# Attention and squared-ReLU FFN on one core: a finer tile of attention weights, named PSUM banks, all engines in program order, a shorter weight conversion and chunk sums on two engines

## The chip, the cores and the metric

One core of one Trainium2 chip (trn2). The metric is the device time of one execution in microseconds, as the median of several runs. All runs here were of state fast: one core runs alone, and the executions of a kernel lay within 0.6% of each other. Engines are called PE (TensorE matmul), PEld (its weight load), DVE (VectorE), ACT (ScalarE), POOL (GpSimd) and SP (SyncE, which here issues the loads and stores).

## The reference, cut to what matters

```python
batch, n_heads, seq, head_dim = (8, 12, 448, 64)          # q, k, v
# attention: RMS norm of q and k with gains g_q, g_k, softmax(q k^T / 8) v
q_n, k_n = (rmsnorm(q, g_q), rmsnorm(k, g_k))
scores = scale * np.matmul(q_n, k_n.transpose(0, 1, 3, 2))
...
x = attn_out.transpose(0, 2, 1, 3).reshape(B * S, H * D)   # 3584 x 768
# FFN
h = np.maximum(x @ w_in, 0.0)                              # 768 x 2048
return (h * h @ w_out).astype(np.float32)                  # 2048 x 768
```

The two FFN weights are float64 in memory. The kernel has to turn them into float32 itself, from pairs of 32-bit words.

## The kernel before

A batch has six pairs of heads, and a pair has four steps (the 448 rows in four chunks of 112). In a step the kernel computes the scores of one chunk for both heads ("weigh": scores on PE, exp on ACT, running sums of the exps on POOL) and one chunk of attention times V for the previous pair ("attend"). Beside this runs the FFN of the previous batch as a stream of "pieces" of 6 or 8 matmul instructions. The program also converts 56 weight chunks, 24 of w_in and 32 of w_out. Only PE is held to program order; a scheduler orders the other engines and assigns buffer slots.

```python
ps_sc = tile_pool(bufs=4, space=PSUM)     # transposes and scores
ps_av = tile_pool(bufs=2, space=PSUM)     # attention times V, and the sums' broadcast "den"
ps_mm = tile_pool(bufs=2, space=PSUM)     # FFN

def weigh(i, m):
    if m == 0:
        for e in range(2):                # one tile per head, all four chunks in it
            weights[i, e] = att.tile([CP, NJ, S], F32, name="wT", tag="wT", bufs=3)
    ...
    for e in range(2):
        sc = ps_sc.tile([CP, S], F32, name="sc", tag="sc")
        nc.tensor.matmul(sc, lhsT=kT[r, ts(m, CP)], rhs=qT[r, :], ...)
    for e, sc in enumerate(scs):
        nc.scalar.activation(weights[i, e][:, m, :], sc, AF.Exp, ...)

def to_float32(dst, low, high):           # 5 passes on DVE, 3 on POOL, 1 on ACT
    ...

with tc.manual_schedule(engines={PE}):
    ...
    for i, (b, c) in enumerate(pairs):
        normalize(i + 1)                  # squares, reduce, rr = ms ** -0.5 on POOL, qn on POOL
        for n in range(NJ):
            weigh(i, n)
            attend(i - 1, n)
            if n == 2: turn(i + 1)        # transposes of Q and K, drained as qT (DVE) and kT (ACT)
            if n == 3: load(i + 2)
            ... FFN pieces, then weight chunks (56 over 36 steps)
```

## Time and profile before

| | before |
|---|---|
| median of the 3 first runs | 1989.45 us |
| PE busy, share of the span | 1755.0 us, 88% |
| DVE, ACT, POOL busy | 496.4, 423.6, 823.0 us |
| mean granted PE clock | 0.932 |
| first FFN matmul starts at | 237.22 us |
| gap in the FFN matmuls at the start of batches 2 to 7 | 21.1 to 24.0 us |

The shares in the first two rows hide two regimes, so they are of little use by themselves. In the start, up to some 400 us, weights are converted and PE waits. Afterwards PE is the limit. The prediction below shows the lines for both. In such lines the first number is the start in us, the second the duration, then engine, source line, operation, written and read tiles, shapes and count; the bracket is the idle time of that engine before it and what ended it.

### The profile page before, as it was taken

How to read it: one execution, taken by the hardware profiler on the slowest of the kernel's cores; microseconds unless marked ns; L12 is line 12 of the kernel's file. 1: busy time of each engine (PE TensorE's matmuls, PEld its weight loads, DVE VectorE, ACT ScalarE, POOL GpSimd, SP SyncE). 2: the span in 40 equal slices, each digit the busy share in tenths (PEclk: the TensorE clock that was granted, in tenths of full speed). 3: DMA queues.
4: the chain of work that ended last, by engine and by line, in shares of the span. 5: the costliest groups of instructions: out<-in, count | busy, mean ns of one | idle time of the engine just before them, and what ended most of it. 6: DMA issues, size and time to landing. Idle time of an engine off the chain costs nothing.

```text
span 1987.5 us, 14446 instructions
## 1 busy us (share of the span) xinstructions
PE 1755.0 (88%) x5440; PEld 800.5 (40%) x5440; DVE 496.4 (25%) x602; ACT 423.6 (21%) x741; POOL 823.0 (41%) x814
## 2 busy tenths in 40 slices
PE   4446767999999999999999999999999999999998
PEld 1111223443444434444444434444444434444555
DVE  5896766212111121112111121112111121011000
ACT  3222212222221122212221122212221122211100
POOL 6988877433432244423442244423442244411200
PEclk8566688999999989999999999999999999999999
DMA  5321223001000110001000110001000110000000
GB/s 170 104 84 51 83 80 86 23 27 44 15 14 22 30 36 24 19 22 39 19 14 22 30 36 23 19 22 39 19 14 22 30 36 24 10 8 17 0 9 26
DMA packets 80532, 70.25 MB, mean 35 GB/s; under 512 B 48196, under 2 KB 69700, under 8 KB 80452
## 3 DMA queue, kind: packets, MB, share of 16 engines
q1 hardware_dynamic: 80128, 69.23, 12.3%
q8 instruction: 45, 0.74, 0.1%
q14 instruction: 35, 0.29, 0.0%
q10 hardware_dynamic: 324, 0.00, 0.0%
HBM read 58.20 MB, written 11.01 MB: 35 GB/s over the span
## 4 chain that ended last, share of the span: by engine, by line
PE 78%; DVE 3%; ACT 2%; POOL 0%; issue 0%; DMA 0%; ACTq 0%; POOLq 0%
PE yps L304 30%; PE hps L275 27%; PE sc L184 10%; PE av L232 8%; PE tr L163 2%; PE den L239 2%; ACT wT L187 2%; DVE qT L165 1%; DVE rden L249 1%; DMA words<-in_moe_w_out_dram 0%; POOL w_out_sb L388 0%; POOL words L387 0%; ACT kT L169 0%; DVE w_out_sb L370 0%; DVE w_out_sb L374 0%
## 5 line engine op out<-in xcount | busy, mean ns | idle before, releaser
L275 PE MATMUL hps<-xT,w_in_sb 128*128 128x448 f32 x1536 | 604.1, 549 | 6.3 <-ACT h L284 6.3
L304 PE MATMUL yps<-w_out_sb,h 128*128 128x384 f32 x1792 | 594.2, 489 | 0.0
L304 PEld LDWEIGHTS yps<-w_out_sb,h 128*128 128x128 f32 x1792 | 335.5, 190 | 255.1 <-issue 35.0
L275 PEld LDWEIGHTS hps<-xT,w_in_sb 128*128 128x128 f32 x1536 | 289.2, 192 | 308.5 <-issue 297.9
L201 POOL TENSOR_TENSOR sum<-sum,wT 112x448 f32<-112x448 f32 x192 | 220.5, 1148 | 349.3 <-ACT wT L187 342.2
L187 ACT ACTIVATE wT<-sc,rr 112x448 f32<-112x448 f32 x384 | 227.6, 633 | 623.5 <-PE sc L184 528.5
L184 PE MATMUL sc<-qT,kT 64*112 64x448 f32 x768 | 284.6, 657 | 68.8 <-ACT wT L187 50.3
L249 DVE RECIPROCAL rden<-den 128x448 f32<-128x448 f32 x48 | 141.9, 2956 | 476.1 <-PE den L239 476.1
L201 POOL TENSOR_TENSOR sum<-wT 112x448 f32<-112x448 f32 x96 | 110.4, 1150 | 313.7 <-PE den L239 222.5
L232 PE MATMUL av<-wT,vt 112*64 112x448 f32 x768 | 209.5, 628 | 0.0
L184 PEld LDWEIGHTS sc<-qT,kT 64*112 64x112 f32 x768 | 78.8, 191 | 245.1 <-ACT wT L187 116.9
L284 ACT ACTIVATE h<-hps 128x448 f32<-128x448 f32 x128 | 69.4, 542 | 373.6 <-PE hps L275 373.6
L137 POOL TENSOR_TENSOR rr<-ms,minus_half 112x16 f32<-112x16 f32 x48 | 141.3, 2943 | 11.7 <-DVE ms L133 10.9
L294 POOL TENSOR_TENSOR h<-h 128x448 f32<-128x448 f32 x64 | 59.5, 932 | 187.7 <-ACT h L284 187.7
L132 DVE TENSOR_REDUCE ms<-squares 112x8 f32<-112x512 f32 x96 | 65.6, 684 | 203.8 <-ACT squares L131 194.8
L289 POOL TENSOR_TENSOR h<-h 128x384 f32<-128x384 f32 x64 | 52.9, 827 | 146.8 <-ACT h L284 146.8
L163 PE MATMUL tr<-ident,qk 112*128 112x112 f32 x192 | 32.1, 295 | 91.5 <-DVE qT L165 91.5
L232 PEld LDWEIGHTS av<-wT,vt 112*64 112x64 f32 x768 | 41.4, 146 | 148.4 <-issue 148.4
L311 DVE COPY y<-yps 128x384 f32<-128x384 f32 x28 | 15.6, 556 | 289.2 <-PE yps L304 289.2
L165 DVE TENSOR_SCALAR qT<-tr,g 128x448 f32<-128x448 f32 x48 | 32.1, 669 | 215.5 <-PE tr L163 215.5
L131 ACT ACTIVATE squares<-qk 112x512 f32<-112x512 f32 x96 | 60.3, 628 | 104.0 <-DMA qk<-in_q_dram 49.6
L253 DVE TENSOR_TENSOR xT<-av,rden 128x448 f32<-128x448 f32 x48 | 29.9, 623 | 200.2 <-PE av L232 177.5
(40 smaller groups left out, 691.7 us busy)
## 6 DMA issues: line engine op xcount, KB each, us to landing
words<-in_moe_w_in_dram SPq DMA_DIRECT2D x24, 512.0 KB, 3.9
words<-in_moe_w_out_dram SPq DMA_DIRECT2D x32, 384.0 KB, 3.1
qk<-in_q_dram SPq DMA_DIRECT2D x48, 224.0 KB, 2.9
vt<-in_v_dram SPq DMA_DIRECT2D x48, 224.0 KB, 2.6
qk<-in_k_dram SPq DMA_DIRECT2D x96, 112.0 KB, 3.1
out_dram<-y SPq DMA_DIRECT2D x8, 336.0 KB, 2.8
out_dram<-y SPq DMA_DIRECT2D x8, 288.0 KB, 2.7
out_dram<-y SPq DMA_DIRECT2D x8, 240.0 KB, 2.6
```

The costliest lines, as they stand in the source:

```text
L131: nc.scalar.activation(squares, qk[:, x], AF.Square)
L132: nc.vector.tensor_reduce(out=ms[:, ts(x, 2 * NJ)], in_=squares, axis=AX.X, op=ALU.add)
L137: nc.gpsimd.tensor_tensor(out=rr.rearrange("p x r -> p (x r)"), in0=ms, in1=minus_half.to_broadcast([CP, 4 * NJ]), op=ALU.pow,)
L163: nc.tensor.transpose(tr[:, ts(j, CP)], rows[:, j].rearrange("p h d -> p (h d)"), ident[:CP, :CP])
L184: nc.tensor.matmul(sc, lhsT=kT[r, ts(m, CP)], rhs=qT[r, :], start=True, stop=True)
L187: nc.scalar.activation(weights[i, e][:, m, :], sc, AF.Exp, scale=normal[i][2][:, 2 * m + e : 2 * m + e + 1])
L201: nc.gpsimd.tensor_tensor(out=sums[i, e], in0=so_far, in1=wT[:, m, :], op=ALU.add)
L232: nc.tensor.matmul(av[ds(e * D, D), :], lhsT=vt[:, e, m, :], rhs=weights[i, e][:, m, :], start=m == 0, stop=m == NJ - 1,)
L249: nc.vector.reciprocal(out=rden, in_=den)
L275: nc.tensor.matmul(ps, lhsT=w_in_sb[:, c, ts(f, P)], rhs=xT[c], start=c == 0, stop=c == NC - 1,)
L284: nc.scalar.activation(h[:, at : at + S], ps, AF.Relu)
L304: nc.tensor.matmul(ps, lhsT=h2[f][:, ts(n, P)], rhs=w_out_sb[:, f, ts(half, HALF)], start=f == 0, stop=f == NF - 1,)
```

## The change

Its intent: PE should find its PSUM banks free, no engine should be ordered by a guess, the weights should cost fewer passes, and POOL should be relieved. It does these things. (The tiles that PE's matmuls write stand in PSUM, which the kernel uses as eight banks of 512 values per partition; the other tiles stand in SBUF.) PSUM tiles become eight named banks. The wT tile is cut into one tile per chunk (12 of them, the same bytes). All engines are held to program order. The weight conversion gets three passes on ACT, one on POOL and three on DVE. The second head's sums go to DVE. V is loaded apart from Q and K, each pair is normalized after its forerunner's first step, and the weight chunks come one per step in batch 0 and three per step after it. Within a step the order is now weight chunks, FFN pieces, weigh, attend, and the FFN stream starts at step 4 of a batch instead of after step 5.

```diff
+    banks = [psum.tile([P, 512], F32, name=f"bank{n}") for n in range(8)]
...
-            tr = ps_sc.tile([P, S], F32, name="tr", tag="sc")
+            tr = banks[2 + x][:, 0:S]
...
+    def new_weights(i, m):
+        for e in range(2):
+            weights[i, e, m] = att.tile([CP, S], F32, name="wT", tag="wT", bufs=3 * NJ)
...
-            sc = ps_sc.tile([CP, S], F32, name="sc", tag="sc")
+        scs = [banks[2 * (m % 2) + e][:CP, 0:S] for e in range(2)]
...
-            nc.gpsimd.tensor_tensor(out=sums[i, e], in0=so_far, in1=wT[:, m, :], op=ALU.add)
+            engine = nc.gpsimd if e == 0 else nc.vector
+            engine.tensor_tensor(out=sums[i, e], in0=so_far, in1=weights[i, e, m], op=ALU.add)
...
+        nc.scalar.activation(high.bitcast(F32), high.bitcast(F32), AF.Copy, scale=REBIAS)
+        nc.scalar.activation(low.bitcast(F32), low, AF.Copy, scale=2.0**-29, bias=2.0**23)
+        nc.scalar.activation(low, low.bitcast(F32), AF.Copy, bias=-(2.0**23))
+        nc.gpsimd.tensor_scalar(out=high.bitcast(F32), ..., op0=ALU.min, op1=ALU.max)
+        nc.vector.tensor_scalar(out=bits, in0=high, ...shift left 4, right 1)
         nc.vector.scalar_tensor_tensor(out=bits, in0=high, scalar=0x80000000, in1=bits, ...)
-        (of the old passes: four on DVE, three on POOL, one on ACT)
+        nc.vector.tensor_tensor(out=bits, in0=bits, in1=low, op=ALU.add)
...
-    with tc.manual_schedule(engines={PE}):
+    with tc.manual_schedule(engines=ENGINES):
...
+                for _ in range(1 if b == 0 else len(chunks) if shift else 3):
+                    if chunks:
+                        load_weights(*chunks.popleft())
+                while ... done * (steps - NJ) < pieces * (step - NJ + 1):
+                    next(stream, None)
                 weigh(i, n)
+                attend(i - 1, n)
+                if n == 0: normalize(i + 1)
                 if n == 2: turn(i + 1)
+                if n == NJ - 1: load_v(i + 1)
```

More of the change, by code (lines that the diff above doesn't have):

```diff
@@ L16 @@
 AX = mybir.AxisListType
-PE = mybir.EngineType.PE
+ENGINES = set(mybir.ALL_ENGINES)
 P = 128
 NJ = 4
-FEW = 2.0**-15
-MOST = (2.0 - 2.0**-3 - 2.0**-23) * 2.0**15 * 2.0
-WEIGHT_STEPS = 36
+REBIAS = 2.0**-112
+MOST = (2.0 - 2.0**-3 - 2.0**-23) * 2.0**-96
 MOST_G = 7.5
@@ L91, in program @@
     ffn_p = ctx.enter_context(tc.tile_pool(name="ffn", bufs=2))
-    ps_sc = ctx.enter_context(tc.tile_pool(name="ps_sc", bufs=4, space=bass.MemoryType.PSUM))
-    ps_av = ctx.enter_context(tc.tile_pool(name="ps_av", bufs=2, space=bass.MemoryType.PSUM))
-    ps_mm = ctx.enter_context(tc.tile_pool(name="ps_mm", bufs=2, space=bass.MemoryType.PSUM))
+    psum = ctx.enter_context(tc.tile_pool(name="psum", bufs=1, space=bass.MemoryType.PSUM))
     ident = const.tile([P, P], F32, name="ident")
@@ L102, in program, with load_qk @@
     w_out_sb = const.tile([P, NF, DM], F32, name="w_out_sb")
+    banks = [psum.tile([P, 512], F32, name=f"bank{n}") for n in range(8)]
     pairs = [(b, c) for b in range(B) for c in range(NPAIR)]
-    loaded, normal, turned, weights, sums, avs, xts = {}, {}, {}, {}, {}, {}, {}
-    def load(i):
+    loaded, values, normal, turned, weights, sums, dens, xts = {}, {}, {}, {}, {}, {}, {}, {}
+    def load_qk(i):
         b, c = pairs[i]
         qk = io.tile([CP, 2, 2 * NJ, D], F32, name="qk", tag="qk")
-        vt = io.tile([CP, 2, NJ, D], F32, name="vt", tag="vt", bufs=3)
-        for dst, src in ((qk[:, 0], q), (vt.rearrange("p h j d -> p (h j) d"), v)):
-            nc.sync.dma_start(
-                dst.rearrange("p (h j) d -> p h (j d)", j=NJ),
-                src[b, 2 * c : 2 * c + 2].rearrange("h (p j) d -> p h (j d)", j=NJ),
-            )
+        nc.sync.dma_start(
+            qk[:, 0].rearrange("p (h j) d -> p h (j d)", j=NJ),
+            q[b, 2 * c : 2 * c + 2].rearrange("h (p j) d -> p h (j d)", j=NJ),
+        )
         for e in range(2):
@@ L122, in load, with load_v @@
             )
-        loaded[i] = qk, vt
+        loaded[i] = qk
+    def load_v(i):
+        b, c = pairs[i]
+        vt = io.tile([CP, 2, NJ, D], F32, name="vt", tag="vt")
+        nc.sync.dma_start(
+            vt.rearrange("p h j d -> p h (j d)"),
+            v[b, 2 * c : 2 * c + 2].rearrange("h (p j) d -> p h (j d)", j=NJ),
+        )
+        values[i] = vt
     def normalize(i):
-        qk = loaded[i][0]
+        qk = loaded.pop(i)
         ms = small.tile([CP, 4 * NJ], F32, name="ms", tag="ms", bufs=2)
@@ L170, in turn @@
         turned[i] = qT, kT
+    def new_weights(i, m):
+        for e in range(2):
+            weights[i, e, m] = att.tile([CP, S], F32, name="wT", tag="wT", bufs=3 * NJ)
     def weigh(i, m):
-        if m == 0:
-            for e in range(2):
-                weights[i, e] = att.tile([CP, NJ, S], F32, name="wT", tag="wT", bufs=3)
         if shift:
             return weigh_shifted(i, m)
+        new_weights(i, m)
         qT, kT = turned[i]
-        scs = []
-        for e in range(2):
+        scs = [banks[2 * (m % 2) + e][:CP, 0:S] for e in range(2)]
+        for e, sc in enumerate(scs):
             r = ds(e * D, D)
-            sc = ps_sc.tile([CP, S], F32, name="sc", tag="sc")
             nc.tensor.matmul(sc, lhsT=kT[r, ts(m, CP)], rhs=qT[r, :], start=True, stop=True)
-            scs.append(sc)
         for e, sc in enumerate(scs):
             nc.scalar.activation(
-                weights[i, e][:, m, :], sc, AF.Exp, scale=normal[i][2][:, 2 * m + e : 2 * m + e + 1]
+                weights[i, e, m], sc, AF.Exp, scale=normal[i][2][:, 2 * m + e : 2 * m + e + 1]
             )
@@ L196, in add_up @@
         for e in range(2):
-            wT = weights[i, e]
             if m == 1:
                 sums[i, e] = att.tile([CP, S], F32, name="sum", tag="sum", bufs=2)
-            so_far = wT[:, 0, :] if m == 1 else sums[i, e]
-            nc.gpsimd.tensor_tensor(out=sums[i, e], in0=so_far, in1=wT[:, m, :], op=ALU.add)
+            so_far = weights[i, e, 0] if m == 1 else sums[i, e]
+            engine = nc.gpsimd if e == 0 else nc.vector
+            engine.tensor_tensor(out=sums[i, e], in0=so_far, in1=weights[i, e, m], op=ALU.add)
     def weigh_shifted(i, m):
+        if m == 0:
+            for n in range(NJ):
+                new_weights(i, n)
         qT, kT = turned[i]
@@ L207, in weigh_shifted @@
             r = ds(e * D, D)
-            sc = ps_sc.tile([CP, S], F32, name="sc", tag="sc")
+            sc = banks[2 * e][:CP, 0:S]
             nc.tensor.matmul(sc, lhsT=qT[r, ts(m, CP)], rhs=kT[r, :], start=True, stop=True)
@@ L213, in weigh_shifted @@
             nc.scalar.activation(w, sc, AF.Exp, bias=nmax)
-            tr = ps_sc.tile([CP, NJ, CP], F32, name="trw", tag="sc")
+            tr = banks[2 * e + 1][:CP, 0:S].rearrange("p (n c) -> p n c", n=NJ)
             for n in range(NJ):
                 nc.tensor.transpose(tr[:, n, :], w[:, ts(n, CP)], ident[:CP, :CP])
-            nc.vector.tensor_copy(out=weights[i, e][:, :, ts(m, CP)], in_=tr)
+            for n in range(NJ):
+                nc.vector.tensor_copy(out=weights[i, e, n][:, ts(m, CP)], in_=tr[:, n, :])
         if m == NJ - 1:
@@ L224, in attend @@
         b, c = pairs[i]
-        vt = loaded[i][1]
-        if m == 0:
-            avs[i] = ps_av.tile([P, S], F32, name="av", tag="av")
-            if c == 0:
-                xts[b] = [None] * NC
-        av = avs[i]
+        vt = values[i]
+        if m == 0 and c == 0:
+            xts[b] = [None] * NC
+        av = banks[4 + i % 2][:, 0:S]
         for e in range(2):
             nc.tensor.matmul(
-                av[ds(e * D, D), :], lhsT=vt[:, e, m, :], rhs=weights[i, e][:, m, :],
+                av[ds(e * D, D), :], lhsT=vt[:, e, m, :], rhs=weights.pop((i, e, m)),
                 start=m == 0, stop=m == NJ - 1,
@@ L236, in attend @@
         if m == 1:
-            den = ps_av.tile([P, S], F32, name="den", tag="av")
+            den = banks[5 - i % 2][:, 0:S]
             for e in range(2):
@@ L249, in attend @@
                 nc.vector.reciprocal(out=rden, in_=den)
-            normal[i] = rden
+            dens[i] = rden
         if m == NJ - 1:
             xT = ffn_p.tile([P, S], F32, name="xT", tag="xT", bufs=NC + 2)
-            nc.vector.tensor_tensor(out=xT, in0=av, in1=normal.pop(i), op=ALU.mult)
+            nc.vector.tensor_tensor(out=xT, in0=av, in1=dens.pop(i), op=ALU.mult)
             xts[b][c] = xT
-            del weights[i, 0], weights[i, 1], turned[i], loaded[i], avs[i]
+            del turned[i], normal[i], values[i]
     left = {}
@@ L272, in ffn @@
         for f in range(NF):
-            ps = ps_mm.tile([P, S], F32, name="hps", tag="mm")
+            ps = banks[6 + f % 2][:, 0:S]
             for c in range(NC):
@@ L301, in ffn @@
             for half in range(2):
-                ps = ps_mm.tile([P, HALF], F32, name="yps", tag="mm")
+                ps = banks[6 + half][:, 0:HALF]
                 for f in range(NF):
@@ L353, in to_float32 @@
     def to_float32(dst, low, high):
+        nc.scalar.activation(high.bitcast(F32), high.bitcast(F32), AF.Copy, scale=REBIAS)
+        nc.scalar.activation(low.bitcast(F32), low, AF.Copy, scale=2.0**-29, bias=2.0**23)
+        nc.scalar.activation(low, low.bitcast(F32), AF.Copy, bias=-(2.0**23))
+        nc.gpsimd.tensor_scalar(
+            out=high.bitcast(F32), in0=high.bitcast(F32), scalar1=MOST, scalar2=-MOST,
+            op0=ALU.min, op1=ALU.max,
+        )
         bits = dst.bitcast(U32)
         nc.vector.tensor_scalar(
-            out=bits, in0=high, scalar1=1, scalar2=1,
-            op0=ALU.logical_shift_left, op1=ALU.logical_shift_right,
-        )
-        nc.gpsimd.tensor_scalar(
-            out=dst, in0=dst, scalar1=MOST, scalar2=FEW, op0=ALU.min, op1=ALU.max
-        )
-        nc.vector.tensor_scalar(
-            out=bits, in0=bits, scalar1=4, scalar2=1,
+            out=bits, in0=high, scalar1=4, scalar2=1,
             op0=ALU.logical_shift_left, op1=ALU.logical_shift_right,
@@ L377, in to_float32 @@
         )
-        nc.vector.tensor_scalar(
-            out=high, in0=bits, scalar1=0x40000000, scalar2=0xFF800000,
-            op0=ALU.bitwise_xor, op1=ALU.bitwise_and,
-        )
-        nc.vector.tensor_scalar(
-            out=bits, in0=bits, scalar1=0x40000000, scalar2=None, op0=ALU.bitwise_xor
-        )
-        power, rest = high.bitcast(F32), low.bitcast(F32)
-        nc.scalar.activation(rest, low, AF.Copy, scale=2.0**-52)
-        nc.gpsimd.tensor_tensor(out=rest, in0=rest, in1=power, op=ALU.mult)
-        nc.gpsimd.tensor_tensor(out=dst, in0=dst, in1=rest, op=ALU.add)
-    load(0)
+        nc.vector.tensor_tensor(out=bits, in0=bits, in1=low, op=ALU.add)
+    load_qk(0)
     for e in range(2):
@@ L399, in program @@
     make_identity(nc, ident)
-    load(1)
-    stream, pieces, done, start = iter(()), 0, 0, 0
+    load_qk(1)
+    load_v(0)
+    steps = NPAIR * NJ
     chunks = deque(weight_chunks())
-    n_chunks = len(chunks)
-    with tc.manual_schedule(engines={PE}):
+    with tc.manual_schedule(engines=ENGINES):
         normalize(0)
         turn(0)
+        stream, pieces, done = iter(()), 0, 0
         for i, (b, c) in enumerate(pairs):
-            if i + 1 < len(pairs):
-                normalize(i + 1)
+            if i + 2 < len(pairs):
+                load_qk(i + 2)
             for n in range(NJ):
+                step = c * NJ + n
+                if step == NJ and b:
+                    stream, pieces, done = ffn(b - 1), ffn_pieces(b - 1), 0
+                for _ in range(1 if b == 0 else len(chunks) if shift else 3):
+                    if chunks:
+                        load_weights(*chunks.popleft())
+                while shift and step == NJ and done < pieces or done * (steps - NJ) < pieces * (step - NJ + 1):
+                    next(stream, None)
+                    done += 1
+                if shift and n == 0 and i:
+                    for m in range(NJ):
+                        attend(i - 1, m)
                 weigh(i, n)
-                if i:
+                if i and not shift:
                     attend(i - 1, n)
-                if n == NJ - 1 and c == 0 and i:
-                    stream, pieces, done = ffn(b - 1), ffn_pieces(b - 1), 0
-                    start = NJ if b > 1 else WEIGHT_STEPS - NPAIR * NJ - 12
+                if n == 0 and i + 1 < len(pairs):
+                    normalize(i + 1)
                 if n == 2 and i + 1 < len(pairs):
                     turn(i + 1)
-                if n == NJ - 1 and i + 2 < len(pairs):
-                    load(i + 2)
-                step = c * NJ + n
-                last = NPAIR * NJ - 1
-                while done * (last - start) < pieces * (step - start):
-                    next(stream, None)
-                    done += 1
-                ready = min(n_chunks, n_chunks * (b * NPAIR * NJ + step + 1) // WEIGHT_STEPS)
-                while n_chunks - len(chunks) < ready:
-                    load_weights(*chunks.popleft())
+                if n == NJ - 1 and i + 1 < len(pairs):
+                    load_v(i + 1)
             if c == NPAIR - 1:
```

## The prediction

> **What bounds the kernel now.** I read the page's slices first. They show two regimes. Up to about 400 us POOL and DVE are loaded and PE is not. After that PE is at 9 in every slice. So I asked for the engines' busy time in four stretches. The first ends where the first FFN matmul starts (237.22 us in PE's timeline). The second ends at 400 us, when the weights are in and PE has filled up. The third ends where the attention of the last batch is done.
>
> ```profile
> core 0: us, PE busy (x) PEld busy (x) DVE busy (x) ACT busy (x) POOL busy (x), PEclk, DMA share, GB/s
> 0.00:237.00 237.00, 115.79 (x296) 36.27 (x296) 178.08 (x228) 65.86 (x115) 195.96 (x167) 0.66 0.33 99
> 237.00:400.00 163.00, 125.47 (x348) 54.73 (x348) 82.48 (x125) 38.73 (x71) 104.39 (x121) 0.85 0.23 64
> 400.00:1840.00 1440.00, 1372.66 (x4390) 631.58 (x4390) 233.60 (x245) 309.51 (x538) 507.81 (x504) 0.98 0.09 24
> 1840.00:1987.00 147.00, 141.11 (x412) 77.91 (x410) 2.23 (x4) 9.47 (x18) 14.80 (x24) 0.99 0.04 12
> ```
>
> Row 1: POOL works 196 of 237 us and DVE 178, PE's clock is 0.66. This is the conversion of the 56 weight chunks (37 of them in batch 0, by the code's 56/36 per step) beside batch 0's attention. Row 3: PE is busy 1373 of 1440 us, so here only PE's own gaps and stretched matmuls can be won. PE's timeline of one ordinary pair shows them:
>
> ```profile
> 866.82 0.97 PE L232 MATMUL av<-wT,vt 112*64 112x448 f32 x4
> 867.73 0.60 PE L163 MATMUL tr<-ident,qn 112*128 112x112 f32 x4
> 869.11 0.60 PE L163 MATMUL tr<-ident,qk 112*128 112x112 f32 x4 [0.78 <-DVE qT L165]
> 869.55 7.92 PE L304 MATMUL yps<-w_out_sb,h 128*128 128x384 f32 x24
> 877.40 1.00 PE L184 MATMUL sc<-qT,kT 64*112 64x448 f32 x2
> 879.12 1.00 PE L184 MATMUL sc<-qT,kT 64*112 64x448 f32 x2 [0.72 <-ACT wT L187]
> 880.06 0.97 PE L232 MATMUL av<-wT,vt 112*64 112x448 f32 x4
> ```
>
> K's transposes wait until Q's have been drained, and the second head's scores wait for the first head's exp. With four score buffers neither should wait. ScalarE's timeline of the same pair gives the reason:
>
> ```profile
> 846.68 0.63 ACT L187 ACTIVATE wT<-sc,rr 112x448 f32<-112x448 f32 x1 [3.03 <-PE sc L184]
> 856.39 0.63 ACT L187 ACTIVATE wT<-sc,rr 112x448 f32<-112x448 f32 x1 [9.09 <-PE sc L184]
> 866.93 0.63 ACT L187 ACTIVATE wT<-sc,rr 112x448 f32<-112x448 f32 x1 [9.90 <-PE sc L184]
> ...
> 878.44 0.63 ACT L187 ACTIVATE wT<-sc,rr 112x448 f32<-112x448 f32 x1 [3.56 <-PE sc L184]
> 881.12 2.21 ACT L187 ACTIVATE wT<-sc,rr 112x448 f32<-112x448 f32 x4 [2.05 <-PE av L232]
> ```
>
> Only one exp runs per step, then four in a row once the previous pair's last av is done. The wT tile holds a head's four chunks and has three buffers for two heads per pair, so the second head's tile is the one that the previous pair still reads. Its scores of three steps sit in three of the four score banks, and everything else shares one. That is my reading of the root: SBUF buffer size, seen as a PSUM shortage.
>
> **What the Trainium skill says.** "Perfetto Trace Analysis", section Optimization Strategy: the same gap repeating on the engine that should be saturated can mean too little SBUF or PSUM for the next tile. The trace agrees: 0.72 and 0.78 us recur in every pair. "PSUM — Partial Sum Buffer", section Engine vs sequencer instructions: ScalarE, VectorE and GpSimd queues are strict FIFO, so program order decides what stands behind a wait. The trace agrees: ScalarE stood 99.0 us in all behind weight DMAs, with exps queued. "SBUF — State Buffer", section Who interferes with whom: a two-port VectorE operation and GpSimd exclude each other. The trace agrees: line 363 on 128x512 took 413 ns at best and 828 at the median. "TensorE: Matmul & The Clock Gate", section What's actually happening: an idle PE falls to half clock. Here the four score matmuls of a step take 1.01 us in the full stage and 1.84 in the sparse one.
>
> **The change, part by part.**
>
> (1) Finer wT tiles (12 of one chunk, same bytes) and fixed banks. A slot now comes back from the attend two steps earlier, and Q's and K's transposes have banks 2 and 3. Saved per ordinary pair: 0.78 us (K's wait), and for the last step's scores 880.06-877.40 = 2.66 us becomes 0.94 (the start-to-start of an undivided pair, 866.82-865.89), so 1.72. Sum 2.5 us. There are five such pairs per batch: 12.5 us.
>
> (2) Start of a batch. The steps before the FFN stream begins are attention alone: six now (steps 0 to 5), four after. PE's timeline has FFN gaps of 24.0, 22.4, 22.7, 21.1, 22.7 and 21.1 us (batches 2 to 7). Six steps at full clock would take 6x1.84 (scores 0.94, av 0.90) + 2x0.85 (den) + 0.95 (transposes) = 13.7, so about 8.7 is lost. After, four steps would take 9.2, but normalize(i+1) is issued in program order after step 0: two exps 1.3, squares 0.63, reduce 0.68, squares, reduce, ms 0.2, rr 2.9, qn 1.05 and hand-overs are about 9.6 us before the transposes, against PE reaching them at 6.4. I lose 3.2 there, 0.6 for kT and an estimated 3 for half clock: 7. Saved 8.7-7 = about 1.7 us. With (1), 14 us per batch, six batches: 84 us. Two pairs of batch 1 add 5. Steady gain: 89 us.
>
> (3) Weight conversion. Removed per chunk: two or three DVE passes and POOL's two 1.0-1.4 us multiplies and adds (lines 387, 388). Left on DVE: a shift as line 363 (0.42 to 0.9), a merge as line 374 (0.68 undisturbed), an add of two tensors, which I take as 0.65: about 1.9 us against 4.65 (0.91+0.90+1.26+0.60+0.99 for 128x512). On POOL one clamp, about 0.85, against 3.57. On ScalarE three passes of 0.65 instead of one. Over 56 chunks DVE falls from 213 us to about 95 and POOL from 168 to about 42. The second head's sums (3 per pair at 1.15 on POOL) go to DVE at about 0.62, the time of line 253's same size: POOL loses 165 us over the kernel, DVE gains 89.
>
> Neither engine is then full in batch 0; the order of the queues is what costs. One pair on DVE (one chunk per step), from one qT to the next: chunk 1.9, sum 0.6 and xT 0.6 after qT (the last two wait for PE, so 4.3 together); then the next pair's first chunk. Its DMA is queued behind load_v, which waits for PE's last av (3.6 after qT at half clock), and behind load_qk: issues 0.45+0.35+1.23, landing about 4.5 later, ScalarE 0.65, POOL 0.85: DVE starts it 11.3 us after qT. Then chunk 1.9, two reduces with a squares between 2.2, ms 0.3; then DVE stands until rr 2.9, qn 1.05 and the next clamp 0.85 have gone through POOL (5); then chunk 1.9, sum 0.6, rden 2.96, chunk 1.9, sum 0.6, qT 0.7. Sum: 11.3+1.9+2.2+0.3+5+8.7 = 29 to 30 us. First chunk on DVE at about 25 us (its DMA now stands behind load_qk(2), issued at 17.8 in the trace), first qT at 40, second at 63 (that chunk's DMA is not held up), fifth of the rest at 63+4x30 = 185: batch 0 ends near 189 us.
>
> Batch 1: 32 chunks of w_out in eleven steps, in two buffers (the y tiles). A buffer's round: DMA 3.1, ScalarE 0.56, POOL 0.6, DVE 0.6+0.65+0.55, hand-overs 0.6 = 6.6, so 3.3 us per chunk, 10 to 12 per step with the pair's stalls. Four steps without FFN to about 237, seven with it to about 320. At 320: step 11, 7x56/20 = 20 FFN pieces. The old kernel at 400: step 16, 35 pieces (192 hps matmuls and 24 yps). The difference is 5 steps (11 us) and 15 pieces at 2.34 (36 us): 47, a little more as the clock recovers, so the new kernel stands there at 370. Gain 30 us.
>
> Sum: 1989.5 - 89 - 30 = 1870.
>
> **The rivals.** (a) The start wins much more: if DMA latency and POOL's chain are hidden better than I laid end to end, batch 0 could run at 24 us per pair and batch 1 at 9 per step: about 50 us more, 1820. For it: DVE's own work is only about 16 us per pair. Against: ScalarE, SP and DVE are now strictly ordered, and each pair has two round trips between them. (b) The start wins nothing or loses: ScalarE has three passes per chunk and every exp and relu stands behind three chunks whose DMA has only two buffers; at 14 us per step the FFN of batch 1 is starved and the 30 us are gone: 1900 to 1920. For it: the 99 us above. (c) Program order puts a new gap of half a microsecond into every step of the full stage (168 steps, 84 us), which would eat (1): about 1950. I went through PE's dependences there (relu two hps back, exp two steps back, y copies, den's sums from the step before) and each producer stands in its own queue before anything later than PE's own place, so I give this little. (d) POOL's relief alone shortens the full stage: no, POOL works 508 of 1440 us there and PE waits for it nowhere.
>
> **Range and chances.** The start is uncertain by some 40 us, the steady part by 20, mostly independent: 1830 to 1915. Two percent faster is below 1949.7; only (c) or a bad (b) misses it.
>
> **What would show each step.** (1) right: no gap before K's transposes, two exps per step, scores always four together; PE's period per batch 199 to 201 and 221 to 223 us instead of 213 and 235. (2) right: FFN gaps near 14 us with a wait of PE's transposes for qn. (3) right: DVE near 95 us for conversion, batch 0 ending near 190, FFN starting near 237 again, ScalarE waiting for weight DMAs. Wrong: hps or yps waiting for ScalarE or DVE in the full stage, or an FFN start later than 260 or earlier than 200.

## The result, and the profile after

The changed kernel takes 1875.73 us (median of 4 runs, 1874.19 to 1879.09); the kernel before took 1991.19 us over the 4 runs of the same series. The ratio is 0.9419, 95% interval 0.9396 to 0.9443: 5.8% faster. A ratio here is the mean time of one kernel's runs over the mean of the other's runs of the same rounds, so it is not quite the ratio of the two medians. The time lies 6 us from the predicted 1870.

The busy times of the engines in four stretches of the changed kernel, cut at the same events as those of before (columns as there):

```profile
core 0: us, PE busy (x) PEld busy (x) DVE busy (x) ACT busy (x) POOL busy (x), PEclk, DMA share, GB/s
0.00:245.00 245.00, 95.58 (x296) 33.17 (x296) 126.49 (x172) 102.65 (x184) 81.88 (x77) 0.63 0.30 93
245.00:380.00 135.00, 113.03 (x340) 49.30 (x338) 62.99 (x93) 58.02 (x113) 54.75 (x68) 0.92 0.27 77
380.00:1726.00 1346.00, 1325.73 (x4399) 623.92 (x4398) 342.10 (x366) 303.55 (x540) 399.55 (x385) 0.98 0.10 26
```

In the first row POOL fell from 196 to 82 us and DVE from 178 to 126, yet the stretch grew from 237 to 245 us. No engine is full there any more: the busiest works 126 of 245 us. In the third row PE is busy 98.5% of the time (1325.73 of 1346), against 95.3% before (1372.66 of 1440).

PE's timeline of an ordinary pair after, to set beside the one of before:

```profile
622.18 0.97 PE L244 MATMUL bank<-wT,vt 112*64 112x448 f32 x4
623.08 0.60 PE L173 MATMUL bank<-ident,qn 112*128 112x112 f32 x4
623.52 0.55 PE L173 MATMUL bank<-ident,qk 112*128 112x112 f32 x4
623.90 10.50 PE L316 MATMUL bank<-w_out_sb,h 128*128 128x384 f32 x32
634.33 1.01 PE L195 MATMUL bank<-qT,kT 64*112 64x448 f32 x4
635.27 0.97 PE L244 MATMUL bank<-wT,vt 112*64 112x448 f32 x4
```

No line has a bracket: K's transposes follow Q's at once, and the four score matmuls run together in 0.94 us from start to start. ACT's timeline of the same stretch has two exps per step, and no run of four:

```profile
622.34 1.16 ACT L197 ACTIVATE wT<-bank,rr 112x448 f32<-112x448 f32 x2 [0.52 <-PE bank L195]
624.11 0.53 ACT L179 COPY kT<-bank 128x448 f32<-128x448 f32 x1 [0.61 <-PE bank L173]
635.37 1.16 ACT L197 ACTIVATE wT<-bank,rr 112x448 f32<-112x448 f32 x2 [10.74 <-PE bank L195]
```

The start of a batch, on PE's timeline:

```profile
686.09 0.60 PE L173 MATMUL bank<-ident,qn 112*128 112x112 f32 x4 [2.97 <-POOL qn L152]
686.53 0.55 PE L173 MATMUL bank<-ident,qk 112*128 112x112 f32 x4
...
687.47 2.06 PE L195 MATMUL bank<-qT,kT 64*112 64x448 f32 x4 [0.40 <-DVE qT L175]
...
689.46 1.76 PE L244 MATMUL bank<-wT,vt 112*64 112x448 f32 x4
```

PE waits 2.97 us for qn, and then the scores take 2.06 us and the av group 1.76 instead of 1.01 and 0.97: the clock has dropped (0.63 of full speed was granted from 686 to 691 us, 1.00 before). The FFN gap is 16.1 to 16.9 us.

One pair of batch 0, on the timeline of all engines (SPq lines are DMA issues):

```profile
96.55 0.68 DVE L175 TENSOR_SCALAR qT<-bank,g 128x448 f32<-128x448 f32 x1
...
97.28 1.84 PE L195 MATMUL bank<-qT,kT 64*112 64x448 f32 x4 [9.65 <-DVE qT L175]
...
100.85 0.33 SPq L129 DMA_DIRECT2D vt<-in_v_dram  x1
...
103.07 1.98 SPq L360 DMA_DIRECT2D words<-in_moe_w_in_dram  x4
...
107.44 0.65 ACT L374 ACTIVATE words<-words 128x512 f32<-128x512 f32 x1 [7.13 <-DMA words<-in_moe_w_in_dram]
...
108.85 0.43 DVE L382 TENSOR_SCALAR w_in_sb<-words 128x512 uint32<-128x512 uint32 x1 [6.77 <-POOL words L377]
...
113.29 2.91 POOL L147 TENSOR_TENSOR rr<-ms,minus_half 112x16 f32<-112x16 f32 x1 [4.47 <-DVE ms L143]
...
117.98 1.35 DVE L382 TENSOR_SCALAR w_in_sb<-words 128x512 uint32<-128x512 uint32 x1 [4.77 <-POOL words L377]
```

This is the loop that the prediction laid end to end: qT, the scores that need it, V's load behind the last av, the next chunks' loads behind V's, ACT, POOL, DVE 11.6 us after qT ended at 97.2; then rr and qn on POOL with DVE standing 4.77 us. From one PE wait for qT to the next a pair takes 31.0, 31.5, 31.9 and 32.4 us.

**Where the time went.** I compare the two at the same state of PE. At 400.84 us the old kernel has done step 15 of batch 1 and 35 FFN pieces. The new one has done step 15 at 380.87 with 34 pieces; the missing piece is 8 matmuls of 0.33 us, so it stands there at 383.5. The start gained 17 us. From there to the end the old kernel takes 1987.5-400.8 = 1586.7 and the new one 1873.4-383.5 = 1489.9 us: 97 us. Sum 114, the difference of the two profiled spans.

### The profile page after: what moved, and what is told of

Its sections match the earlier page's. It is cut to its first block, busy times and chain, and to the rows that moved or that the text cites. A ratio compares the mean times of both kernels' runs of the same rounds, so it can differ in the third digit from the quotient of the medians.

```text
span 1873.4 us, 14405 instructions
## 1 busy us (share of the span) xinstructions
PE 1675.4 (89%) x5440; PEld 784.3 (42%) x5440; DVE 533.8 (28%) x634; ACT 473.6 (25%) x853; POOL 551.7 (29%) x558
## 3 DMA queue, kind: packets, MB, share of 16 engines
q1 hardware_dynamic: 80128, 69.23, 13.2%
## 4 chain that ended last, share of the span: by engine, by line
PE 80%; issue 5%; DVE 4%; POOL 4%; DMA 3%; ACT 2%; SPq 1%; POOLq 0%; ACTq 0%; DVEq 0%
PE bank L316 31%; PE bank L287 30%; PE bank L195 8%; PE bank L244 7%; POOL rr L147 2%; DMA words<-in_moe_w_out_dram 2%; PE bank L173 2%; PE bank L251 1%; DMA words<-in_moe_w_in_dram 1%; DVE rden L261 1%; POOL words L377 1%; DVE sum L211 1%; ACT words L374 1%; DVE w_in_sb L386 1%; DVE w_in_sb L382 1%
## 5 line engine op out<-in xcount | busy, mean ns | idle before, releaser
L287 PE MATMUL bank<-xT,w_in_sb 128*128 128x448 f32 x1536 | 612.1, 554 | 22.0 <-ACT h L296 20.7
L316 PE MATMUL bank<-w_out_sb,h 128*128 128x384 f32 x1792 | 593.9, 489 | 0.0
L316 PEld LDWEIGHTS bank<-w_out_sb,h 128*128 128x128 f32 x1792 | 335.5, 190 | 253.9 <-issue 32.2
L287 PEld LDWEIGHTS bank<-xT,w_in_sb 128*128 128x128 f32 x1536 | 291.4, 194 | 335.3 <-issue 287.6
L197 ACT ACTIVATE wT<-bank,rr 112x448 f32<-112x448 f32 x384 | 221.9, 629 | 553.9 <-PE bank L195 549.4
L195 PE MATMUL bank<-qT,kT 64*112 64x448 f32 x768 | 219.3, 638 | 101.2 <-DVE qT L175 70.6
L211 POOL TENSOR_TENSOR sum<-sum,wT 112x448 f32<-112x448 f32 x96 | 111.9, 1165 | 410.8 <-ACT wT L197 410.0
L211 DVE TENSOR_TENSOR sum<-sum,wT 112x448 f32<-112x448 f32 x96 | 109.8, 1143 | 421.3 <-ACT wT L197 421.3
L244 PE MATMUL bank<-wT,vt 112*64 112x448 f32 x768 | 200.8, 605 | 0.0
L261 DVE RECIPROCAL rden<-bank 128x448 f32<-128x448 f32 x48 | 141.5, 2948 | 1.2 <-PE bank L251 1.2
L211 POOL TENSOR_TENSOR sum<-wT 112x448 f32<-112x448 f32 x48 | 71.0, 1479 | 75.9 <-PE bank L251 74.9
L323 DVE COPY y<-bank 128x384 f32<-128x384 f32 x28 | 15.3, 548 | 229.8 <-PE bank L316 229.8
```

The costliest lines, as they stand in the source:

```text
L195: nc.tensor.matmul(sc, lhsT=kT[r, ts(m, CP)], rhs=qT[r, :], start=True, stop=True)
L197: nc.scalar.activation(weights[i, e, m], sc, AF.Exp, scale=normal[i][2][:, 2 * m + e : 2 * m + e + 1])
L211: engine.tensor_tensor(out=sums[i, e], in0=so_far, in1=weights[i, e, m], op=ALU.add)
L244: nc.tensor.matmul(av[ds(e * D, D), :], lhsT=vt[:, e, m, :], rhs=weights.pop((i, e, m)), start=m == 0, stop=m == NJ - 1,)
L261: nc.vector.reciprocal(out=rden, in_=den)
L287: nc.tensor.matmul(ps, lhsT=w_in_sb[:, c, ts(f, P)], rhs=xT[c], start=c == 0, stop=c == NC - 1,)
```

## The experiments

Twelve kernels ran, all correct, all timed in three rounds beside the kernel before (median 1989.35 to 1990.27 us in the three series). "FFN start" is the first FFN matmul and "gap" the FFN gap at the starts of the later batches, both from PE's timeline.

| kernel | median us | ratio to before [95%] | FFN start us | gap us |
|---|---|---|---|---|
| before | 1989 to 1991 | 1 | 237.2 | 21.1 to 24.0 |
| changed | 1875.73 | 0.9419 [0.9396, 0.9443] | 245.5 | 16.1 to 16.9 |
| b_wt | 1823.02 | 0.9146 [0.9116, 0.9175] | 215.7 | 13.4 |
| b_conv | 1903.68 | 0.9548 [0.9520, 0.9577] | 181.5 | 22.4 to 23.9 |
| b_wtconv | 1747.71 | 0.8788 [0.8773, 0.8803] | 164.3 | 13.4 |
| a_pools | 1816.41 | 0.9113 [0.9083, 0.9143] | 202.5 | 13.8 to 16.2 |
| a_flip | 1817.80 | 0.9138 [0.9122, 0.9153] | 204.6 | 13.8 to 16.2 |
| a_pe | 1754.69 | 0.8804 [0.8775, 0.8833] | 150.5 | 13.2 to 14.8 |
| a_sumpool | 1869.76 | 0.9383 [0.9352, 0.9414] | 239.8 | 16.1 to 16.9 |
| a_oldconv | 1912.12 | 0.9595 [0.9566, 0.9623] | 259.8 | 15.9 to 16.9 |
| a_norm | 1866.10 | 0.9365 [0.9336, 0.9394] | 240.6 | 15.9 to 16.1 |
| a_spread | 1837.72 | 0.9218 [0.9191, 0.9245] | 246.8 | none |
| a_pe_fs | 1737.44 | 0.8737 [0.8723, 0.8752] | 155.0 | none |
| a_order_best | 1742.36 | 0.8761 [0.8747, 0.8776] | 169.7 | none |

The labels say what they start from: b_ is the kernel before with a part of the change, a_ is the changed kernel with a part altered.

### b_wt: the finer wT tiles alone

```diff
-            weights[i, e] = att.tile([CP, NJ, S], F32, name="wT", tag="wT", bufs=3)
+            weights[i, e, m] = att.tile([CP, S], F32, name="wT", tag="wT", bufs=3 * NJ)
```
(and the uses of it; pools, order and conversion as before)

> The kernel before with one part of the change alone: the wT tiles cut to one chunk each (12 of them, same bytes); PSUM pools, conversion, sums and order of the engines stay as before. Theory (the second head's wT tile comes back too late and its scores hold the banks): the waits of 0.72 us (scores for exp) and 0.78 us (K's transposes for qT) go from the full stage, two exps per step; 2.5 us per ordinary pair, about 12.5 per batch plus some at the batch starts, so 80 to 95 us: 1895 to 1910 us. Rival (the rotating PSUM pool is at fault and fixed banks are needed): gaps stay, 1975 to 1995 us.

Measured: 1823.02 us, 167 us below before and 53 us below the whole change. The direction was the theory's, the size almost double its 80 to 95 us. The start of a batch on PE's timeline:

```profile
666.20 0.60 PE L163 MATMUL tr<-ident,qn 112*128 112x112 f32 x4
666.64 0.55 PE L163 MATMUL tr<-ident,qk 112*128 112x112 f32 x4
667.11 1.01 PE L186 MATMUL sc<-qT,kT 64*112 64x448 f32 x4
```

The rotating pools deliver three bank pairs in a row without a wait. The gap at a batch start is 13.4 us with the old six steps of attention, just the 13.7 us that the prediction worked out for them at full clock. So the 8.7 us that it saw lost there came from wT too. The start of one batch's FFN to that of the next takes 191.1 or 211.8 us, against 214.1 and 233.1 to 234.4: 22.2 us per batch on average. The start gained as well: from 504.0 to 461.6 us at the FFN start of batch 2, 42 us. The sum 42+124 (the rest of the spans, 1483.5 against 1360.0) is the 166 us of the profiled spans. Named banks and program order were not needed for any of it.

### a_pools: the changed kernel with rotating PSUM pools

```diff
-    banks = [psum.tile([P, 512], F32, name=f"bank{n}") for n in range(8)]
+    ps_sc, ps_av, ps_mm pools as before, with 4, 2 and 2 buffers
```

> The changed kernel with the eight named banks put back into the three rotating PSUM pools (4, 2 and 2 buffers), all else as changed. Theory: with fine wT tiles the pools rotate without waits, so within 10 us of the changed kernel, 1868 to 1886 us. Rival (named banks remove the gaps): the 0.7 and 0.8 us gaps come back and about 85 us with them, 1945 to 1965 us.

Measured: 1816.41 us, 59 us faster than the changed kernel. Both theories fell: the banks do not save, and they are not neutral; they cost. FFN starts at 202.5 instead of 245.5 us, so most of it lies in batch 0. A pool hands out four banks in turn. Scores of step 1, scores of step 2, transposes and scores of step 3 alternate between the two halves. The named version gives the scores of step m the pair m % 2, so those of step 3 take banks 2 and 3, the very banks in which Q's transposes wait for DVE to drain qT. In batch 0 DVE reaches qT late, and the score matmuls of step 3, the last av, V's load and the next chunks' loads queue up behind it (the pair shown above: 9.65 us of PE waiting).

### a_flip: named banks, dealt out in the order of use

```diff
-            tr = banks[2 + x][:, 0:S]
+            tr = banks[2 * (i % 2) + x][:, 0:S]
-        scs = [banks[2 * (m % 2) + e][:CP, 0:S] for e in range(2)]
+        scs = [banks[2 * ((i + (m == 1)) % 2) + e][:CP, 0:S] for e in range(2)]
```

> The changed kernel with its named banks dealt out otherwise: Q's and K's transposes and the score pairs alternate between the two bank pairs in the order of use, so that the last step's scores of a pair no longer need the banks that qT is drained from. Theory (the pools run was 60 us faster because in batch 0 the last step's scores, the last av and so load_v and the next chunk DMAs stood behind qT; 24 instead of 31.5 us per pair): as with pools, 1808 to 1824 us, FFN start near 202 us. Rival (the pools win in some other way, through waits released earlier than by named tiles): 1855 to 1880 us.

Measured: 1817.80 us and FFN start 204.6: as with pools. It is which bank, not named against pooled. PE's timeline in batch 0:

```profile
78.42 1.01 PE L195 MATMUL bank<-qT,kT 64*112 64x448 f32 x4
79.36 0.97 PE L244 MATMUL bank<-wT,vt 112*64 112x448 f32 x4
90.57 1.84 PE L195 MATMUL bank<-qT,kT 64*112 64x448 f32 x4 [10.23 <-DVE qT L175]
```

PE still waits for qT, but now with the scores of the next pair, which use qT as data. The last av of the pair is done at 80 us, ahead of the wait, so the loads behind it go out early. The next such wait ends at 114.47 us: a pair takes 23.9 us instead of 31 to 32.

### b_conv and b_wtconv: the conversion alone, and with wT

```diff
     def to_float32(dst, low, high):
-        (the old nine passes)
+        (the new seven passes)
```

> The kernel before with the new weight conversion alone. Its batch 0 had GpSimd busy 196 of 237 us; the new conversion takes 2.7 us of GpSimd and 2.7 us of VectorE work off each of 37 chunks there. Theory (the engines' work bounded the old start, and it is the program order that let the changed kernel keep only about 17 us of that): here the FFN starts 40 to 80 us earlier than 237 us, and the kernel takes 1910 to 1955 us. Rival (chunk buffers and DMA bound the old start): FFN start within 15 us of 237, 1970 to 1995 us.

Measured: 1903.68 us, 86 us faster, a little more than the theory's range. FFN starts at 181.5, 56 us earlier. So the engines' work did bound the old start.

> The kernel before with two parts of the change, the fine wT tiles and the new conversion, and nothing of the named banks, the program order or the split sums. Theory (these two carry the whole gain and the rest costs): the two gains of 167 and 86 us nearly add up, 1730 to 1765 us, FFN start near 150 us, gaps at the batch starts near 13.4 us. Rival (both shorten the same stretch of the start, so they do not add): 1785 to 1820 us.

Measured: 1747.71 us. The parts give 167 and 86 us alone and 242 us together, so they nearly add up. Two parts of the change, a few lines each, are worth more than twice the whole. The rest (banks, order, sums, the new order within a step, the FFN start, V's load, the place of normalize, the pace of the chunks) costs 1875.7-1747.7 = 128 us. Of these only the banks, the engines' order and the sums have runs of their own below; what the others cost is not shown.

### a_oldconv: the changed kernel with the old conversion

```diff
     def to_float32(dst, low, high):
-        (the new seven passes)
+        (the old nine passes)
```

> The changed kernel with the old weight conversion. Theory (in program order a chunk's passes lie end to end, so the shorter chain of the new one is what makes program order bearable): a pair of batch 0 goes from 31 to 32 us to about 45 to 55, a chunk of w_out from 3.3 to 5 us or more: 100 to 180 us slower, 1975 to 2055 us. Rival (DMA landing and the rr and qn chain bound the start, not the passes): less than 40 us slower, 1880 to 1915 us.

Measured: 1912.12 us, 36 us slower: the rival was right and my 100 us and more were wrong. FFN start moves by 14 us only, and the first matmul with w_out from 373.8 to 407.9 us. The new conversion is worth 86 us where queues are free and 36 us in program order, where chunk loads and the chain through rr and qn set the pace.

### a_pe: only PE in program order

```diff
-    with tc.manual_schedule(engines=ENGINES):
+    with tc.manual_schedule(engines={mybir.EngineType.PE}):
```

> The changed kernel with only PE in program order, the other engines ordered by the scheduler as before. Theory (program order is neutral in the full stage and costs time in the start, where VectorE and GpSimd stand behind DMA and the rr and qn chain): start shorter by 20 to 60 us, full stage the same, 1815 to 1860 us. Rival (program order brings part of the gain): slower than the changed kernel, 1890 to 1940 us, with waits of PE for ScalarE or VectorE in the full stage.

Measured: 1754.69 us, 121 us faster than the changed kernel. The theory's direction held and its 20 to 60 us were too few. FFN starts at 150.5 us, 95 us earlier, with the bad bank choice still in. DVE is busy 115 of the first 150 us (126 of 245 in program order). Program order brings nothing in the full stage either; it costs some 20 us there, where the theory had none: from the first w_out matmul to the end a_pe takes 1751.9-272.8 = 1479 us and the changed kernel 1873.4-373.8 = 1500.

### a_sumpool: all sums on POOL

```diff
-            engine = nc.gpsimd if e == 0 else nc.vector
+            engine = nc.gpsimd
```

> The changed kernel with all chunk sums on GpSimd again. Theory: in the full stage nothing waits for GpSimd, and in batch 0 the sums are not on the chain from qT to qT, so 0 to 10 us slower, 1872 to 1886 us. Rival (the split carries part of the gain because GpSimd was the full engine of the start): 20 us or more slower, 1895 us and up.

Measured: 1869.76 us; its ratio's interval (0.9352 to 0.9414) overlaps the changed kernel's, so the split sums save nothing, and may cost a little. The groups of the changed kernel by line (busy us, mean ns of one, then idle time before):

```profile
L211 POOL TENSOR_TENSOR sum<-sum,wT 112x448 f32<-112x448 f32 x96 | 111.9, 1165 | 410.8 <-ACT wT L197 410.0
L211 DVE TENSOR_TENSOR sum<-sum,wT 112x448 f32<-112x448 f32 x96 | 109.8, 1143 | 421.3 <-ACT wT L197 421.3
L211 POOL TENSOR_TENSOR sum<-wT 112x448 f32<-112x448 f32 x48 | 71.0, 1479 | 75.9 <-PE bank L251 74.9 <-ACT wT L197 1.0
L211 DVE TENSOR_TENSOR sum<-wT 112x448 f32<-112x448 f32 x48 | 35.2, 734 | 228.6 <-PE bank L251 227.5 <-ACT wT L197 1.1
```

The prediction took 0.62 us for a sum on DVE. Sums of two steps out of three average 1.14 us there (second line); in most of them the partner on POOL had started 0.41 us before. The first sums of a pair (third and fourth line) mostly start on both engines at once: there DVE's takes 0.63 us and POOL's 1.61 (medians), where POOL alone took 1.13 in the kernel before.

### a_norm: normalize one step earlier at a batch start

```diff
-                if n == 0 and i + 1 < len(pairs):
+                if n == 0 and (c or not i) and i + 1 < len(pairs):
                     normalize(i + 1)
+                if n == NJ - 1 and c == NPAIR - 1 and i + 2 < len(pairs):
+                    normalize(i + 2)
```

> The changed kernel, but the pair that follows the first pair of a batch is normalized one step earlier (last step of the batch before, still under FFN matmuls). Theory (the FFN gap of 16.1 us at each batch start is the 9.6 us chain squares, reduce, rr, qn, which PE's transposes wait for 3.0 us, and the half clock after it): the wait for qn goes, gap 9.5 to 11.5 us, six batches: 28 to 40 us faster, 1836 to 1848 us. Rival (half clock comes from the lack of FFN work itself, not from the wait): gap 13 to 14 us, 12 to 20 us faster, 1856 to 1864 us.

Measured: 1866.10 us, gap 15.9 to 16.1. Neither answer came, since the edit does not do what I wrote. In the changed kernel a step begins with its FFN pieces, so a normalize at the end of the batch's last step stands behind all of them: the last FFN matmul ends at 667.3 and squares begins at 669.3 us. The chain was moved ahead by one attention step, and the wait for qn fell from 2.97 to 2.08 us only. Of the 10 us in the total, 5 lie before the FFN start (240.6 against 245.5), which this edit hardly touches; a_sumpool, in another series, starts its FFN as early (239.8), so differences of this size between series are not read. This run tells nothing about the theory.

### a_spread: the FFN stream stretched over the batch start

```diff
-                while ... done * (steps - NJ) < pieces * (step - NJ + 1):
+                while done < due(pieces, (step - NJ) % steps):   # w_in pieces at the old pace,
+                                                                  # the others up to step 3 of the next batch
-            if c == NPAIR - 1:
-                for _ in stream: pass
```

> The changed kernel, but the second half of each FFN stream is stretched over the first four steps of the next batch, so that these have FFN matmuls too. Theory: no FFN gap over 3 us is left, no wait for qn, full clock; the work at full clock of a gap is 9.2 us of 16.1, so 6 to 7 us for each of six batches: 36 to 42 us faster, 1834 to 1840 us. Rival (something else, such as xT or h tiles not yet free, takes the gap's place): under 20 us faster, above 1856 us.

Measured: 1837.72 us, 38 us faster than the changed kernel and inside the range. No FFN gap is left after batch 1, PE waits for nothing after 374 us, and its clock there is 1.00. This settles that the loss at a batch start goes when PE has FFN work beside the chain through rr and qn. How much of the loss was the wait for qn and how much the lower clock, no run separates.

### a_pe_fs and a_order_best: two ways to a faster kernel

a_pe_fs is the changed kernel with the edits of a_pe, a_flip and a_spread.

> The changed kernel with only PE in program order, the alternating banks and the FFN stream stretched over the batch start: meant to beat both kernels. Theory (the three act on different places: queue order in the start, banks in the start, batch starts): 1755 minus 30 to 36 for the batch starts (five or six gaps of 14 us with 9.2 of work at full clock in them) minus 5 to 15 for the banks, 1705 to 1722 us. Rival (with free queues the banks no longer matter and the stretched stream meets late xT tiles): 1735 to 1755 us.

Measured: 1737.44 us, the fastest of all, 7.4% below the changed kernel by the medians, but 15 us above its range and inside the rival's. The stretches of this kernel (columns as above):

```profile
0.00:274.00 274.00, 187.23 (x613) 75.08 (x614) 179.15 (x267) 157.10 (x298) 157.92 (x145) 0.86 0.41 122
274.00:1588.00 1314.00, 1314.00 (x4418) 616.71 (x4417) 341.53 (x363) 306.14 (x539) 422.81 (x389) 1.00 0.10 27
```

From 274 us on PE is busy all the time at full clock; there is nothing left there but PE's own work. Stretching the stream took 18 us off that part (1479 to 1461 us from the first w_out matmul to the end), not 30: I had taken six gaps' surplus over 9.2 us each, and about 12 us of it I cannot place. The banks gave nothing here (FFN start 155.0 against 150.5), as the rival had it; its other half, late xT tiles, did not come, for PE waits for nothing after 274 us. That DVE drains qT early with free queues is my reading.

a_order_best keeps full program order but changes the program:

```diff
-        to_float32(dst, words[:, :, 0], words[:, :, 1])        # right behind its own load
+        issued.append((dst, words[:, :, 0], words[:, :, 1]))   # loads up to 4 chunks ahead
...
                 attend(i - 1, n)
+                convert(1 if b == 0 else 2)                    # passes behind the step's attention
...
-                if n == NJ - 1 and i + 1 < len(pairs): load_v(i + 1)
+                if n == 1 and i: load_v(i)
```
(with the edits of a_flip and a_spread)

> The changed kernel in full program order, but with its program reordered: chunk DMAs issued up to four chunks ahead, a chunk's passes placed after the step's attention, two chunks a step in batch 1, V loaded a pair later, alternating banks, stretched FFN stream. Theory (program order costs only by what the program puts ahead of what): a pair of batch 0 falls to about 18 to 20 us, FFN starts at 140 to 165 us, no FFN gap at batch starts; 1690 to 1740 us. Rival (strict queues on every engine cost in the start whatever the order): FFN start above 185 us, 1770 us or more.

Measured: 1742.36 us, 2 us outside the range; a pair of batch 0 takes 22.1 us (waits for qT end at 62.29, 84.39 and 106.51 us), not 18 to 20, and FFN starts at 169.7. Still, in full program order this is 133 us faster than the changed kernel. Of the 95 us that a_pe takes off the FFN start, this kernel gets 76 in full program order. So most of what the change lost in the start it lost by what its program puts ahead of what and by its banks. How much of the 22.1 us strict queues still cost I did not separate.

## Why the prediction was right, point by point

**(1) The gaps of an ordinary pair.** Right in cause and effect. The wT tile with three buffers was the root (b_wt), the waits of 0.78 and 0.72 us are gone, and exps come in twos. The fixed banks that (1) named beside it were not: a_pools is 59 us faster without them, for in batch 0 banks 2 and 3 put the last scores of a pair behind qT (24 us per pair in a_flip, 31 to 32 here). The prediction took that place of the last av as given and did not see that the bank choice made it. Two more things were left out: the same tile also cost the old kernel its 8.7 us per batch start and 42 us up to the FFN start of batch 2. The change as a whole does not show that, because its other parts take it back.

**(2) The batch start.** The working was right: 9.2 us of work plus a loss of 7 is 16.2, and 16.1 to 16.9 was measured, with the predicted wait for qn (2.97 us against 3.2) and the dropped clock. The sign that I listed for it, a gap near 14 us, did not follow from that working and was wrong. (1) and (2) together were to save 14 us per batch. From FFN start to FFN start the five full periods saved 15.3, 16.0, 14.4, 16.1 and 14.4 us, on average 15.2. The steady part saved 97 us against 89.

**(3) The start.** The mechanism was right: the engines are no longer full, and the order of the queues sets the pace. Laid end to end the wait after qT was to be 11.3 us and the wait behind rr and qn 5; they were 11.6 and 4.77. (Two sums of the prediction have slips: the terms of the 11.3 add up to 11.6, and 63+4x30 is 183, not 185.) Mis-sized were the passes on DVE. The chunk behind rr and qn took 3.9 us (117.98 to 121.92), not 1.9, and the sum after it 1.05, not 0.6, with POOL's clamps and sums running at the same moment; over the kernel the three passes took 110 us of DVE, not 95. So a pair took 31 to 32.4 us instead of 29 to 30, and FFN started at 245.5 instead of 237. The seven steps of batch 1 after that took 91.5 us (245.5 to 337.1) instead of 83, with the 20.7 us of waits for relu of rival (b) in them. The gain was 17 us, not 30.

**The rivals.** (a) did not happen in this kernel, but b_wtconv and a_pe show that the room was there: FFN starts at 150 to 164 us once queues or passes are not in each other's way. (b) went half way: PE did stand 20.7 us for relu behind chunk conversions in batch 1. (c) did not happen: PE had only 20.3 us of waits between 330 us and the end. (d) was rightly turned down, as far as the sums go: a_sumpool puts their work back on POOL and is not slower.

So the steady part came out 8 us better than predicted and the start 13 us worse, and that the total lies within 6 us is partly luck. It was right as a sum of a larger gain and a larger loss. The prediction knew of the loss in the start, but it set the new start only against the old one. The comparison that would have shown its size, the new conversion without the new order, was not made before the result; b_conv and b_wtconv made it after.

## What to carry to other kernels

When PE waits for a PSUM bank, look for who holds the other banks and what that one waits for; here the cause was an SBUF tile whose release was too coarse, and cutting it by chunk, at no cost in bytes, was the largest gain. Try each part of a compound change alone before keeping it: two of these parts gave 242 us and the others took 128 back. Program order on every engine turns the source order into the schedule, so a load or a pass that waits must not stand ahead of work that is ready, and a fixed bank must not be shared by two uses of which one is drained late.

## What the Trainium skill lacked or had wrong

- "Perfetto Trace Analysis", section Optimization Strategy: right that a repeated gap can mean too few buffers. It does not say that the scarce buffer may lie in the other memory: here PSUM waits of 0.72 and 0.78 us came from SBUF tiles, and b_wt, which changes only those, saved 167 us.
- "SBUF — State Buffer", section Who interferes with whom: says that a VectorE instruction with two SBUF inputs contends with a GpSimd one that reads SBUF, and that the second fully blocks. The trace nearly agrees: where POOL's 112x448 sum had started 0.41 us before, DVE's has a median of 1202 ns, against 617 with no POOL instruction beside it. But the two sums together take 1.61 us, less than the 1.13 and 0.62 of each alone added up, so the second was held for most of the first and not for all of it. Splitting the sums over the two engines therefore shortens them little. That this is why the split saved nothing (a_sumpool) is not shown, for PE waits for no sum in the changed kernel.
- "VectorE: DVE Perf Modes", section Specifications: says integer operands are converted and exact only below 2^24. The whole-number add of 512 uint32 words appears in the trace as an operation on 128x1024 uint16 that takes 0.69 us undisturbed, with correct results in every run that has it. No page that I found gives this form or its time.
- No page that I found gives a time for a power on GpSimd. The rr operation on only 112x16 values took 2.9 us at the least in every run (median 2.9, but 3.3 in a_pe and a_pe_fs), and it stands in the chain of every pair.
